# Attention tiles of the first batch pair loaded in 2 KB runs and turned by 64x64 products, in a chunked attention and low-rank mixer kernel

## The chip, the cores and the metric

The kernel runs on one core of a Trainium2 chip. The metric is the device time of one execution in microseconds (us), taken as the median of repeated runs; lower is better.

## What is computed

Eight batches (B) of eight heads (H), 576 tokens (S) and 64 channels per head (D). Attention works within chunks of 64 tokens; then a mixer works on the 512 channels (DM) of each token:

```python
# attention, per batch, head and chunk of 64 tokens
scores = q_c @ k_c.T / sqrt(64)
x = softmax(scores) @ v_c                    # heads side by side: x is [8, 576, 512]
# mixer
u = x + ((x.transpose(0, 2, 1) @ U) @ V).transpose(0, 2, 1)      # U is 576x32, V is 32x576
out = u + maximum(u @ w_ch1, 0) @ w_ch2      # w_ch1 is 512x2048, w_ch2 is 2048x512
```

q, k and v arrive as float32; U, V and the two weight matrices arrive as float64 words, and the kernel turns them into a high and a low part in fp32r.

## The kernel before

Two batches make a pair (`pr`), 1152 tokens, nine tiles of 128 tokens; three tiles make a group (`g`). Per pair and group there are 16 blocks (`f`, one for each 128 of the 2048 hidden channels): `hidden` (L823, 12 products of 384 columns), a relu split into a high part on ACT (L831, `hh`) and a low part on DVE (L836, `hl`), and `project_out` (L849, 9 products of 512 columns). There are 192 blocks in all, and TensorE does them one behind the other, the `out` of a block behind the `hidden` of the next.

**The planned part** is everything up to the 32nd block: groups 0 and 1 of the first pair in six stretches (`STRETCHES`), and all that must come before them. `LEAD` names the items in order of rank: `U` and `V` (the low-rank matrices), `W0` to `W15` (load and conversion of a weight slice: three steps on ACT, four on DVE), `T0` to `T8` (attention of the nine tiles of the first pair), `P0` and `P1` (x times U for either batch), `M0` and `M1` (mixes of groups 0 and 1), `S` (the split of U). `order()` is a list scheduler in Python with a cost for each operation and the rooms of the buffers; it gives one order per engine, and each engine works its own list strictly in order. DMAs are issued from SP (q, k, the second chunk of v, the weights), POOL (the first chunk of v, U, V) and ACT (`permute`).

**A planned tile** (`attention_ops`, L424 on): q and k arrive as [128 tokens, 8 heads, 64], so each run in DRAM is 256 B. Four products with the identity (L432, transpose mode, 128x128) turn each; ACT copies the result from PSUM (L442). Even heads end in the upper 64 partitions, odd heads in the lower. Then 16 scores products of 64x64 (L450, the two partition halves into two PSUM banks), maximum and subtraction on DVE, exp on ACT, four transposes of the weights, 16 products with v (L481; a column of ones in v, set by POOL at L410, gives the sums), and the scaling on DVE (L499). The buffers of q, k, v and of the turned q and k come from the tag `w`, which has 16 places and is shared with the weights.

**The agenda.** The tiles of the next pairs, and the third group (tiles 6 to 8) of the first, are worked in by hand at numbered slots, four to a block, so that slot 128 (`FIRST`) is the end of the planned part. `Tile` needs q and k in another order in DRAM, which `permute` (L655) writes: 16 DMAs of 288 KB for the second pair, each tied to the end of a `hidden` of the planned part (`gate`), here blocks 5 to 12 and every second of 14 to 28. `Tile.load` (L672) reads eight of them, and the first is at slot 68. `Mix` (L765 on) adds the low-rank term (L610, L616), turns 32x32 squares on DVE (L785), writes them to DRAM with four DMAs (`put`, L793), reads them back (`get`, L799), and splits them (L812 on ACT, L813 on DVE). The third group's mixes are at slots 97, 99 and 101 (`low_rank`, `add`), one slot later the turn, then `put`, and `get` at 102, 104 and 106; the splits are at 111 to 113.

Of the kernel before, what the change touches and what calls it, by code (L numbers as in the profile page):

```python
# [10 lines left out]
F32 = mybir.dt.float32  # L11
# [10 lines left out]
def kernel(  # L22
# [11 lines left out]
    nc = tc.nc  # L34
    B, H, S, D = q.shape
# [29 lines left out]
    work = ctx.enter_context(tc.tile_pool(name="work", bufs=1))  # L65
# [46 lines left out]
    def wslot(shape, dtype, name):  # L112
        return wpool.tile([P, *shape], dtype, tag="w", name=name, bufs=NF)
# [18 lines left out]
    def transfer(run, kb, *after, eng="SP", us=0.62, take="", free="", gbs=190.0):  # L132
        q = "dq" if eng == "SP" else "pq"
        o = Op(eng, us, run, *after, take=take + " " + q, lat=1.2 if eng == "SP" else 2.9)
        return Op("DMA", kb * 1.024 / gbs, lambda: None, o, free=free + " " + q, lat=0.5)

    ROOM = {"bank": 8, "w": NF, "slot": NS, "x": NX, "y": 2, "ut": 2, "h": 2, "mx": 2, "sm": 2, "dq": 8, "pq": 8}
    TICK = 3.4133

    def order():  # L140
        free_at = {}
# [9 lines left out]
        while ready:  # L151
# [238 lines left out]
    def early(pr, t):  # L390
        return pr == 0 and t < NEARLY

    loaded = {}
    begun = {}
    x_of = {}
# [1 line left out]
    ut_of = {}  # L397

    def load(pr, t, z):
        n = f"{pr}_{t}"  # L400
        if z == "q":
            if early(pr, t):
                words = wslot((4 * DM,), F32, "qkv_" + n)
                qn, kn = (words[:, z * DM : (z + 1) * DM].rearrange("p (h d) -> p h d", h=H) for z in range(2))
                vn = words[:, 2 * DM : 2 * DM + H * D1].rearrange("p (c a k) -> p c a k", c=2, k=D1)
            else:
                qn = slot(F32, "qn_" + n, (P, H, D))
                kn = slot(F32, "kn_" + n, (P, H, D))
                vn = slot(F32, "vn_" + n, (P, 2, HP, D1))
            nc.gpsimd.memset(vn[:, :, :, D:], 1.0)  # L410
            loaded[pr, t] = qn, kn, vn
        if z != "v":
            dst, src = (loaded[pr, t][0], q) if z == "q" else (loaded[pr, t][1], k_in)
            for r, m, b, s0 in segments(pr, t):
                nc.sync.dma_start(dst[r : r + m], src[b, :, s0 : s0 + m, :].rearrange("h s d -> s h d"))

    def load_v(pr, t, c, e):
        b, s0 = divmod(t * P + c * C, S)
        (nc.gpsimd if early(pr, t) and c == 0 else nc.sync).dma_start(
            loaded[pr, t][2][e * C : (e + 1) * C, c, :, 0:D],  # L420
            v[b + 2 * pr, e::2, s0 : s0 + C, :].rearrange("h s d -> s h d"),
        )

    def attention_ops(pr, t, after=None):  # L424
        n = f"{pr}_{t}"
        st = {}
        mine = early(pr, t)

        def transpose(src, name):
            ps = st[name] = bank("ps_" + name + n)  # L430
            for j in range(4):
                nc.tensor.transpose(ps[:, j * P : (j + 1) * P], src[:, j * P : (j + 1) * P], ident)  # L432

        def evacuate(name):
            if name[0] == "e" or not mine:
                dst = slot(F32, name + n, (P, HP, P))
            elif name[0] == "q":
                st["qk"] = wslot((2, HP, P), F32, "qkT_" + n)
                dst = st["qk"][:, 0]
            else:  # L440
                dst = st["qk"][:, 1]
            nc.scalar.copy(dst.rearrange("p a b -> p (a b)"), st[name])  # L442
            st[name] = dst

        def scores():
            ps = [bank(f"sc{e}_{n}") for e in range(2)]
# [48 lines left out]

        def scaled(e):
            if e == 0:
                st["x"] = work.tile([P, HP, 2, D], F32, tag="x", name="x_" + n, bufs=NX)
            nc.vector.tensor_mul(  # L499
                st["x"][:, :, e, :],  # L500
                st["av"][e][:, :, 0:D],
                st["sm"][:, e].unsqueeze(2).broadcast_to([P, HP, D]),
            )
            if e == 1:
                x_of[pr, t] = st["x"].rearrange("p a b k -> p (a b k)")

        src = lambda z: loaded[pr, t][z].rearrange("p h d -> p (h d)")
        flat = lambda: st["ex"].rearrange("p a b k -> p (a b k)")
        lq = transfer(lambda: load(pr, t, "q"), 256, after, take="w" if mine else "slot slot slot")
        lk = transfer(lambda: load(pr, t, "k"), 256, lq.after[0])  # L510
        lv, lq0 = lk, lq.after[0]
        vs = []
        for c in range(2):
            for e in range(2):
                lv = transfer(
                    lambda c=c, e=e: load_v(pr, t, c, e),
                    64,
                    (lk.after[0] if mine else lv.after[0]) if c else lq0,
                    eng="SP" if c or not mine else "POOL",
                )  # L520
                vs.append(lv)
        tq = Op("PE", 0.45, lambda: transpose(src(0), "qT_"), lq, begun.get((pr, t - 2)), take="bank")
        cq = Op("ACT", 0.48, lambda: evacuate("qT_"), tq, take="w" if mine else "slot", free="bank")
        tk = Op("PE", 0.45, lambda: transpose(src(1), "kT_"), lk, tq, take="bank")
        ck = Op("ACT", 0.48, lambda: evacuate("kT_"), tk, cq, take="" if mine else "slot", free="bank")
        sc = Op("PE", 0.58, scores, ck, take="bank bank", free="w" if mine else "slot slot slot slot")
# [5 lines left out]
        te = Op("PE", 0.45, lambda: transpose(flat(), "eT_"), ex, take="bank", free="slot")  # L532
        ce = Op("ACT", 0.48, lambda: evacuate("eT_"), te, take="slot", free="bank")
        av = Op("PE", 0.6, values, ce, *vs, take="bank bank x", free="slot w" if mine else "slot slot")
# [365 lines left out]

    LEAD = "U W0 T0 T1 T2 T3 T4 P0 T5 T6 V T7 T8 P1 M0 M1 W1 W2 W3 W4 W5 W6 S W7 W8 W9 W10 W11 W12 W13 W14 W15"
# [9 lines left out]
    for item in LEAD.split():  # L913
        rank[0] += 1
        z, i = item[0], int(item[1:] or 0)
# [51 lines left out]
    FIRST = 2 * NF * 4  # L967

    def at(s, *runs):
        agenda.setdefault(s, []).extend(runs)  # L970
# [8 lines left out]
        at(s + 6, a.get_ex)  # L979
        return a  # L980

    def plan_mix(pr, t, s):
        m = Mix(pr, t)
        at(s, m.low_rank, m.add)
        at(s + 1, m.turn)
        at(s + 2, m.put)
        at(s + 5, m.get)
        if pr:
            at(s + 10, m.split)
        return m  # L990

    def plan_proj(pr, e, i, s):
        if i == 0:
# [37 lines left out]
    for pr in range(1, NPAIR):  # L1031
# [5 lines left out]
        s = made[pr, 4] + 1  # L1037
# [4 lines left out]
        s = made[pr, 8] + 1  # L1042
# [68 lines left out]
```

## Time and profile before

| | us |
|---|---|
| median of 3 runs (938.71 to 943.48) | 943.03 |
| the profiled execution, its own time | 941.59 |
| its span, first to last instruction | 939.8 |

Of the span TensorE is busy 913.7 us (97%), VectorE (DVE) 457.9, ScalarE (ACT) 228.1, GpSimd (POOL) 82.2. The chain of work that ended last is TensorE for 91%; 84% of it are the two product lines of the blocks, L823 and L849. "Busy" counts a product from its start to its modelled end, so a busy TensorE need not be at its full rate, and what a stage costs beyond its products has to be read from the order of the products in that stage.

### The profile page before, as it was taken

What the parts mean: (1) busy time and instruction counts of PE and PEld (TensorE: products, weight loads), DVE (VectorE), ACT (ScalarE), POOL (GpSimd) and SP (SyncE); (2) the same over time, 40 slices, a digit from 0 to 9 for tenths busy, and PEclk for the clock granted to TensorE, in tenths of its full rate; (3) what the DMA queues carried; (4) which work ended last, traced back from release to release, by engine and by line L of the source; (5) the groups of instructions that cost most, each with busy time, mean ns of one, the idle gap of its engine ahead of it and who ended that gap; (6) DMA issues with size and microseconds to landing.
All of it is one profiled execution on the core that took longest, in us unless ns stands there. A gap on an engine that the chain in (4) does not pass through costs nothing.

```text
span 939.8 us, 16349 instructions
## 1 busy us (share of the span) xinstructions
PE 913.7 (97%) x6596; PEld 807.5 (86%) x6596; DVE 457.9 (49%) x901; ACT 228.1 (24%) x399; POOL 82.2 (9%) x147
## 2 busy tenths in 40 slices
PE   3999999989999999999999999999999999999998
PEld 2769888878888888888898888889899889999997
DVE  3788995555544555544534455543541533321211
ACT  4565771111221212211111122111221121111110
POOL 6000002021120101110010111120120100000000
PEclk9999999999999999999999999999999999999999
DMA  9984875464385574423455665531350312200000
GB/s 190 178 314 120 198 199 97 91 167 118 80 185 126 110 164 118 107 57 82 114 113 113 124 120 132 139 80 36 100 135 1 91 23 68 78 23 1 34 1 34
DMA packets 281211, 100.10 MB, mean 107 GB/s; under 512 B 206544, under 2 KB 268528, under 8 KB 281136
## 3 DMA queue, kind: packets, MB, share of 16 engines
q1 hardware_dynamic: 165440, 76.19, 32.2%
q10 hardware_dynamic: 111360, 14.16, 9.6%
q0 software_dynamic: 4336, 8.71, 3.7%
q8 instruction: 52, 0.85, 0.4%
q14 instruction: 23, 0.19, 0.1%
HBM read 74.63 MB, written 38.54 MB: 120 GB/s over the span
## 4 chain that ended last, share of the span: by engine, by line
PE 91%; DMA 4%; DVE 2%; SPq 1%; ACT 1%; issue 1%; ACTq 0%; DVEq 0%; POOL 0%
PE o L849 42%; PE h L823 42%; PE as L750 2%; DMA qkv<-in_k_dram 2%; PE as L697 1%; DMA wraw<-in_moe_w_ch_dram 1%; PE u L610 1%; PE y L564 1%; PE y L563 1%; DVE x L861 1%; PE y L569 1%; DMA kn<-kblocks 0%; DVE wraw L101 0%; DMA xs<-xb 0%; PE sc L450 0%
## 5 line engine op out<-in xcount | busy, mean ns | idle before, releaser
L823 PE MATMUL h<-uth,w 128*128 128x384 f32 x1536 | 424.0, 338 | 0.0
L849 PE MATMUL o<-w,hh 128*128 128x512 f32 x1152 | 364.1, 397 | 0.0
L836 DVE SCALAR_TENSOR_TENSOR hl<-h,hh 128x384 fp32r<-128x384 f32 x192 | 106.9, 557 | 382.3 <-ACT hh L831 382.2
L823 PEld LDWEIGHTS h<-uth,w 128*128 128x128 f32 x1536 | 281.2, 188 | 8.1 <-issue 0.2
L823 PE MATMUL h<-utl,w 128*128 128x384 f32 x768 | 259.6, 338 | 0.0
L849 PEld LDWEIGHTS o<-w,hh 128*128 128x128 f32 x1152 | 212.5, 188 | 35.3 <-ACT hh L831 0.4
L849 PE MATMUL o<-w,hl 128*128 128x512 f32 x576 | 227.9, 396 | 5.4 <-DVE hl L836 5.4
L831 ACT ACTIVATE hh<-h 128x384 fp32r<-128x384 f32 x192 | 94.3, 491 | 532.9 <-PE h L823 525.2
L823 PEld LDWEIGHTS h<-utl,w 128*128 128x128 f32 x768 | 144.2, 188 | 8.4 <-DVE utl L635 0.5
L849 PEld LDWEIGHTS o<-w,hl 128*128 128x128 f32 x576 | 108.4, 188 | 33.0 <-DVE hl L836 7.6
L687 POOL DMA_DIRECT2D vn<-in_v_dram x108 | 65.8, 616 | 649.6 <-DVE qT L680 131.3
L717 ACT ACTIVATE ex<-ex 128x512 f32<-128x512 f32 x27 | 17.1, 633 | 100.6 <-DVE ex L711 94.9
L710 DVE TENSOR_REDUCE mx<-as 128x4 f32<-128x256 f32 x54 | 22.7, 420 | 31.3 <-PE as L697 31.2
L861 DVE TENSOR_TENSOR x<-o,x 128x512 f32<-128x512 f32 x48 | 30.5, 679 | 5.1 <-PE o L849 5.1
L616 DVE TENSOR_TENSOR x<-u,x 128x512 f32<-128x512 f32 x36 | 23.9, 670 | 7.5 <-PE u L610 7.5
L813 DVE TENSOR_TENSOR utl<-uf,uth 128x512 fp32r<-128x512 f32 x30 | 20.4, 681 | 10.9 <-ACT uth L812 10.9
L711 DVE TENSOR_TENSOR ex<-as,mx 128x256 f32<-128x256 f32 x54 | 22.9, 425 | 1.9
L750 PEld LDWEIGHTS as<-vn,eT 64*64 64x64 f32 x864 | 15.4, 137 | 9.3 <-issue 9.3
L785 DVE STREAM_TRANSPOSE xb<-x 128x512 f32<-128x512 f32 x30 | 21.2, 706 | 0.6
L812 ACT CAST uth<-uf 128x512 fp32r<-128x512 f32 x30 | 18.2, 614 | 12.8 <-DMA uf<-xs 12.8
L556 DVE TENSOR_TENSOR xl<-x,xh 128x512 fp32r<-128x512 f32 x30 | 20.1, 681 | 1.0 <-ACT xh L552 0.7
L680 DVE STREAM_TRANSPOSE qT<-qn 128x512 f32<-128x512 f32 x27 | 18.9, 700 | 3.2 <-DMA qn<-qblocks 3.2
(87 smaller groups left out, 518.3 us busy)
## 6 DMA issues: line engine op xcount, KB each, us to landing
wraw<-in_moe_w_ch_dram SPq DMA_DIRECT2D x32, 512.0 KB, 5.3
out_dram<-x SPq DMA_DIRECT2D x36, 256.0 KB, 2.2
xs<-xb SPq DMA_DIRECT2D x120, 64.0 KB, 2.0
uf<-xs SPq DMA_DIRECT2D x30, 256.0 KB, 2.7
qblocks<-in_q_dram ACTq DMA_DIRECT2D x24, 288.0 KB, 4.3
kblocks<-in_k_dram ACTq DMA_DIRECT2D x24, 288.0 KB, 4.3
vn<-in_v_dram POOLq DMA_DIRECT2D x108, 64.0 KB, 2.8
exs<-exb SPq DMA_DIRECT2D x108, 64.0 KB, 1.8
```

The source lines that it names most:

```text
L616: nc.vector.tensor_add(x, st["u"], x)
L687: nc.gpsimd.dma_start(self.vn[e * C : (e + 1) * C, c], v[b + 2 * self.pr, HP * e : HP * (e + 1), s0 : s0 + C, :].rearrange("h s d -> s h d"),)
L710: nc.vector.reduce_max(mx[:, e], self.sc[e].rearrange("p (h k) -> p h k", k=C), axis=AX.X)
L711: nc.vector.tensor_sub(self.ex[:, e].rearrange("p b h k -> p h b k"), self.sc[e].rearrange("p (h b k) -> p h b k", b=2, k=TB), mx[:, e].un ...
L750: nc.tensor.matmul(ps[e][cs, (HP + hp) * C : (HP + hp + 1) * C], lhsT=self.eT[rows, hp, 2 * c : 2 * c + 2, :].rearrange("p a i -> p (a i)" ...
L785: nc.vector.transpose(self.xb.rearrange("p g (c t) -> p c g t", t=TB), x_of[self.pr, self.t].rearrange("p (c g k) -> p c g k", g=NQ, k=TB),)
L813: nc.vector.tensor_sub(ul, self.uf, uh)
L823: nc.tensor.matmul(ps[:, :GN], lhsT=w[:, z, cc], rhs=u[:, cc, :], start=(n == 0), stop=(n == 3 * NCC - 1))
L831: nc.scalar.activation(hh, ps[:, :GN], AF.Relu)
L836: nc.vector.scalar_tensor_tensor(hl, ps[:, :GN], 0.0, hh, op0=ALU.max, op1=ALU.subtract)
L849: nc.tensor.matmul(acc[j], lhsT=h[:, js], rhs=w2[f][:, z], start=(first and i == 0), stop=(final and i == 2),)
L861: nc.vector.tensor_add(x, ps, x)
```

## The change

1. q and k of a planned tile are loaded with partition = (head, run of 8 tokens), so that each partition is one contiguous run of 8 x 64 floats, 2 KB. For eight heads and 16 runs the DRAM side of the DMA has dimensions 8, 16 and 512. Tile 4, which spans two batches, takes two loads of 64 partitions for each.
2. They are turned by 16 products of 64x64 with the identity for each of q and k (no transpose mode), the upper 64 partitions to the upper half of the output and the lower to the lower, both halves into the same PSUM bank; the copy on ACT reads this bank with a permutation. Heads 0 to 3 are now in the upper half and 4 to 7 in the lower; v is loaded and x is laid out to match.
3. The planner's costs: 340 GB/s for these loads instead of 190, 0.55 us for a turn instead of 0.45.
4. The order `LEAD` is another one: T0 to T2 come first, W0 moves behind T5, S behind W8.
5. The 16 `permute` DMAs are tied to blocks 9 to 18 and to every second of 20 to 30.
6. The third group's mixes are at slots 83, 85 and 87 instead of 97, 99 and 101, with `get` at 103 to 105; the splits stay.
7. `early` is gone: it was true for all nine planned tiles.

```diff
-    NEARLY = 9
+    RUN = 8
+    LONG = 340.0
...
     def load(pr, t, z):
-            nc.sync.dma_start(dst[r : r + m], src[b, :, s0 : s0 + m, :].rearrange("h s d -> s h d"))
+            nc.sync.dma_start(
+                dst[r : r + m], src[b, :, s0 : s0 + m, :].rearrange("h (i j) d -> h i (j d)", j=RUN)
+            )
...
     def load_v(pr, t, c, e):
-            v[b + 2 * pr, e::2, s0 : s0 + C, :].rearrange("h s d -> s h d"),
+            v[b + 2 * pr, HP * e : HP * (e + 1), s0 : s0 + C, :].rearrange("h s d -> s h d"),
...
-            for j in range(4):
-                nc.tensor.transpose(ps[:, j * P : (j + 1) * P], src[:, j * P : (j + 1) * P], ident)
+            for j in range(RUN):
+                cs = slice(j * D, (j + 1) * D)
+                for e in range(2):
+                    if whole:
+                        rows = slice(e * C, (e + 1) * C)
+                        nc.tensor.matmul(ps[rows, cs], lhsT=src[rows, cs], rhs=ident[rows, rows], start=True, stop=True)
+                        continue
+                    nc.tensor.matmul(
+                        ps[e * C : (e + 1) * C, cs].rearrange("p (a c i) -> p c a i", a=HP, c=2),
+                        lhsT=src[:, cs],
+                        rhs=ident.rearrange("p (c b i) -> p c b i", c=2, b=2)[:, :, e],
+                        start=True,
+                        stop=True,
+                    )
...
+    def ordered(name):
+            nc.scalar.copy(
+                dst.rearrange("p a (i j) -> p a i j", j=RUN),
+                st[name].rearrange("p (j a i) -> p a i j", j=RUN, a=HP),
+            )
...
-    LEAD = "U W0 T0 T1 T2 T3 T4 P0 T5 T6 V T7 T8 P1 M0 M1 W1 W2 W3 W4 W5 W6 S W7 W8 ..."
+    LEAD = "T0 T1 T2 V T3 U T4 T5 W0 T6 T7 P0 T8 P1 M0 M1 W1 W2 W3 W4 W5 W6 W7 W8 S ..."
...
-            if 4 < blocks < 13 or blocks in range(14, 30, 2):
+            if 8 < blocks < 19 or blocks in range(20, 32, 2):
...
     for t in range(6, 9):
-        m = plan_mix(0, t, FIRST - 31 + 2 * (t - 6))
-        at(FIRST - 17 + t - 6, m.split)
+        plan_mix(0, t, FIRST - 45 + 2 * (t - 6), FIRST - 25 + t - 6)
```

## Rows read from the trace of the kernel before

**Rows 1.** The page: the span in 40 slices of 23.5 us, busy tenths of TensorE and of DVE.

```profile
PE   3999999989999999999999999999999999999998
...
DVE  3788995555544555544534455543541533321211
```

**Rows 2.** The windows view, all engines: window in us, its length, then busy us (and instructions) of PE, PEld, DVE, ACT and POOL, the granted TensorE clock (1.00 is full speed), DMA share, GB/s.

```profile
15.00:20.00 5.00, 2.18 (x9) 1.79 (x10) 2.70 (x3) 1.33 (x3) 2.81 (x7) 1.00 1.23 173
20.00:25.00 5.00, 4.06 (x46) 3.20 (x45) 3.50 (x8) 4.37 (x10) 1.34 (x3) 1.00 1.31 177
...
50.00:60.00 10.00, 9.57 (x150) 6.38 (x140) 8.36 (x26) 6.78 (x11) 0.00 (x0) 1.00 1.03 364
...
80.00:100.00 20.00, 18.53 (x94) 16.37 (x93) 16.97 (x22) 11.93 (x14) 0.00 (x0) 1.00 0.70 165
...
180.00:200.00 20.00, 17.57 (x128) 15.29 (x130) 8.16 (x14) 3.62 (x7) 2.44 (x4) 0.95 0.72 192
200.00:250.00 50.00, 49.77 (x444) 44.11 (x437) 29.47 (x68) 10.37 (x19) 7.31 (x12) 0.98 0.43 103
```

**Rows 3.** Waits, 0 to 30 us: who waited for whom, us in total, times, longest.

```profile
PE ps_qT L432 <- DMA qkv<-in_q_dram: 11.9, 2, 8.2
```

**Rows 4.** The instructions of the tile that holds q, k and v, to 60 us: the last line of that answer, the time from a DMA's issue to its landing.

```profile
DMA to landing us min/median/max: 2.6/6.2/11.5
```

**Rows 5.** Timeline of the lead-in (start, us, engine, line, operation; a bracket gives the idle time before it): the first load of q and its turn, the last tile's load of k and its turn, two of the copies on ACT, and products of the mix.

```profile
1.77 0.43 SPq L415 DMA_DIRECT2D qkv<-in_q_dram  x1
...
8.22 1.09 PE L432 MATMUL ps_qT<-ident,qkv 128*128 128x128 f32 x4 [8.22 <-DMA qkv<-in_q_dram]
...
35.04 0.58 ACT L442 COPY qkT<-ps_qT 128x512 f32<-128x512 f32 x1
...
42.63 0.58 SPq L415 DMA_DIRECT2D qkv<-in_k_dram  x1
...
50.18 0.66 PE L432 MATMUL ps_kT<-ident,qkv 128*128 128x128 f32 x4
...
53.81 0.94 PE L610 MATMUL u<-ys,vst 128*128 128x512 f32 x3
...
56.07 1.47 PE L622 MATMUL ut<-ident,x 128*128 128x128 f32 x12
```

**Rows 6.** The chain of waits followed back from 110 us (start, us, what): what one group of products takes when products stand right before and behind it, and where the blocks become continuous.

```profile
29.70 0.63 PE av L481 x32
...
31.39 0.62 PE sc L450 x32
32.01 0.69 PE vall L304 x4
...
34.43 0.44 PE ps_kT L432 x4
...
44.02 0.59 PE ps_eT L432 x4
...
45.04 0.86 PE y L569 x2
...
68.56 0.69 PE o L849 x3
69.25 4.22 PE h L823 x24
```

**Rows 7.** Timeline of ACT, 80 to 110 us: the issue of `permute` DMAs, and the conversion step behind them.

```profile
86.88 3.89 ACTq L655 DMA_DIRECT2D qblocks<-in_q_dram  x1
90.88 1.12 ACT L91 ACTIVATE wroom<-wraw 128x1024 f32<-128x1024 f32 x1 [3.95 <-issue]
```

**Rows 8.** Waits of TensorE alone, 80 to 100 us and then 180 to 200 us.

```profile
PE o L849 <- DVE hl L836: 1.5, 1, 1.5
PE o L849 <- DVE hl L836: 2.4, 1, 2.4
```

**Rows 9.** The chain of waits followed back from 260 us, the stretch around slots 100 to 113.

```profile
186.44 3.69 DMA xs<-xb
...
190.60 0.52 SPq L672
...
191.17 4.29 DMA kn<-kblocks
...
196.84 0.48 DVE hl L836
...
197.37 1.40 PE o L849 x4
```

**Rows 10.** Timelines of SP and of DVE, 154 to 180 us: the get of the first `Tile`'s weights (slot 83), the load of the second `Tile` (slot 86) and its turn on DVE (slot 91), then an `add` and a turn of the third group's mixes and the first `put`.

```profile
156.04 2.21 SPq L742 DMA_DIRECT2D eT<-exs  x4
158.30 0.53 SPq L672 DMA_DIRECT2D qn<-qblocks  x1
...
178.22 1.76 SPq L793 DMA_DIRECT2D xs<-xb  x4
166.10 0.70 DVE L680 STREAM_TRANSPOSE qT<-qn 128x512 f32<-128x512 f32 x1
...
178.11 0.65 DVE L616 TENSOR_TENSOR x<-u,x 128x512 f32<-128x512 f32 x1
178.80 0.71 DVE L785 STREAM_TRANSPOSE xb<-x 128x512 f32<-128x512 f32 x1
```

More of the change, by code (lines that the diff above doesn't have):

```diff
@@ L399, in load @@
     def load(pr, t, z):
-        n = f"{pr}_{t}"
         if z == "q":
[L402 to L409, printed above, removed]
-            nc.gpsimd.memset(vn[:, :, :, D:], 1.0)
-            loaded[pr, t] = qn, kn, vn
@@ L412, in load @@
-        if z != "v":
-            dst, src = (loaded[pr, t][0], q) if z == "q" else (loaded[pr, t][1], k_in)
-            for r, m, b, s0 in segments(pr, t):
-                nc.sync.dma_start(dst[r : r + m], src[b, :, s0 : s0 + m, :].rearrange("h s d -> s h d"))
+            words = wslot((4 * DM,), F32, f"qkv_{pr}_{t}")
+            vn = words[:, 2 * DM : 2 * DM + H * D1].rearrange("p (c a k) -> p c a k", c=2, k=D1)
+            nc.gpsimd.memset(vn[:, :, :, D:], 1.0)
+            loaded[pr, t] = words[:, 0:DM], words[:, DM : 2 * DM], vn
@@ L417, in load_v @@
+        dst, src = (loaded[pr, t][0], q) if z == "q" else (loaded[pr, t][1], k_in)
+        for r, m, b, s0 in segments(pr, t):
+            nc.sync.dma_start(
+                dst[r : r + m], src[b, :, s0 : s0 + m, :].rearrange("h (i j) d -> h i (j d)", j=RUN)
+            )
     def load_v(pr, t, c, e):
         b, s0 = divmod(t * P + c * C, S)
-        (nc.gpsimd if early(pr, t) and c == 0 else nc.sync).dma_start(
+        (nc.gpsimd if c == 0 else nc.sync).dma_start(
             loaded[pr, t][2][e * C : (e + 1) * C, c, :, 0:D],
-            v[b + 2 * pr, e::2, s0 : s0 + C, :].rearrange("h s d -> s h d"),
+            v[b + 2 * pr, HP * e : HP * (e + 1), s0 : s0 + C, :].rearrange("h s d -> s h d"),
@@ L422, in load_v, with attention_ops, by_heads, turned @@
         )
-    def attention_ops(pr, t, after=None):
+    def attention_ops(pr, t):
         n = f"{pr}_{t}"
         st = {}
-        mine = early(pr, t)
-        def transpose(src, name):
+        def by_heads(src, name):
             ps = st[name] = bank("ps_" + name + n)
+            whole = len(list(segments(pr, t))) == 1
+            for j in range(RUN):
[13 more added lines that the diff above has]
+        def ordered(name):
+            if name[0] == "q":
+                st["qk"] = wslot((2, HP, P), F32, "qkT_" + n)
+            dst = st["qk"][:, "qk".index(name[0])]
+            nc.scalar.copy(
+                dst.rearrange("p a (i j) -> p a i j", j=RUN),
+                st[name].rearrange("p (j a i) -> p a i j", j=RUN, a=HP),
+            )
+            st[name] = dst
+        def turned():
+            ps = st["eT_"] = bank("ps_eT_" + n)
+            src = st["ex"].rearrange("p a b k -> p (a b k)")
@@ L431, in transpose, with evacuate @@
             for j in range(4):
                 nc.tensor.transpose(ps[:, j * P : (j + 1) * P], src[:, j * P : (j + 1) * P], ident)
[L434 to L443, printed above, removed]
+        def evacuate():
+            dst = slot(F32, "eT_" + n, (P, HP, P))
+            nc.scalar.copy(dst.rearrange("p a b -> p (a b)"), st["eT_"])
+            st["eT_"] = dst
@@ L497, in scaled @@
             if e == 0:
-                st["x"] = work.tile([P, HP, 2, D], F32, tag="x", name="x_" + n, bufs=NX)
+                st["x"] = work.tile([P, 2, HP, D], F32, tag="x", name="x_" + n, bufs=NX)
             nc.vector.tensor_mul(
-                st["x"][:, :, e, :],
+                st["x"][:, e],
                 st["av"][e][:, :, 0:D],
@@ L504, in scaled @@
             if e == 1:
[L505 to L511, printed above, removed]
+                x_of[pr, t] = st["x"].rearrange("p b a k -> p (b a k)")
+        lq = transfer(lambda: load(pr, t, "q"), 256, take="w", gbs=LONG)
+        lk = transfer(lambda: load(pr, t, "k"), 256, lq.after[0], gbs=LONG)
         vs = []
@@ L517, in attention_ops @@
                     64,
-                    (lk.after[0] if mine else lv.after[0]) if c else lq0,
-                    eng="SP" if c or not mine else "POOL",
+                    lk.after[0] if c else lq.after[0],
+                    eng="SP" if c else "POOL",
                 )
                 vs.append(lv)
[L522 to L526, printed above, removed]
+        tq = Op("PE", 0.55, lambda: by_heads(loaded[pr, t][0], "qT_"), lq, begun.get((pr, t - 2)), take="bank")
+        cq = Op("ACT", 0.48, lambda: ordered("qT_"), tq, take="w", free="bank")
+        tk = Op("PE", 0.55, lambda: by_heads(loaded[pr, t][1], "kT_"), lk, tq, take="bank")
+        ck = Op("ACT", 0.48, lambda: ordered("kT_"), tk, cq, free="bank")
+        sc = Op("PE", 0.58, scores, ck, take="bank bank", free="w")
         m0 = Op("DVE", 0.42, lambda: maximum(0), sc, take="slot mx")
@@ L531, in attention_ops @@
         ex = Op("ACT", 0.53, exp, s1)
-        te = Op("PE", 0.45, lambda: transpose(flat(), "eT_"), ex, take="bank", free="slot")
-        ce = Op("ACT", 0.48, lambda: evacuate("eT_"), te, take="slot", free="bank")
-        av = Op("PE", 0.6, values, ce, *vs, take="bank bank x", free="slot w" if mine else "slot slot")
+        te = Op("PE", 0.45, turned, ex, take="bank", free="slot")
+        ce = Op("ACT", 0.48, evacuate, te, take="slot", free="bank")
+        av = Op("PE", 0.6, values, ce, *vs, take="bank bank x", free="slot w")
         sm = Op("DVE", 0.52, sums, av, take="sm")
@@ L980, in plan_tile, with plan_mix @@
         return a
-    def plan_mix(pr, t, s):
+    def plan_mix(pr, t, s, get=None):
         m = Mix(pr, t)
@@ L986, in plan_mix @@
         at(s + 2, m.put)
[L987 to L990, printed above, removed]
+        at(s + 5 if get is None else get, m.get)
+        at(s + 10 if get is None else get + 8, m.split)
     def plan_proj(pr, e, i, s):
```

4 lines of the change are left out of this document (1 added, 3 removed).

## The prediction

> **What bounds the kernel now.** I read the page's slices first [rows 1]: TensorE is at 9 tenths or more nearly everywhere, so only where it is not can much be won. That is the first slice, and within it the windows [rows 2] show TensorE busy for 2.2 us of 15 to 20 and 4.1 us of 20 to 25, while the DMA engines are at their full share and move only 173 to 177 GB/s. The waits [rows 3] name the cause: TensorE waits 11.9 us in two waits for q. So the lead-in is bound by loads of short runs; the first q is issued at 1.77 and turned at 8.22, the last k is issued at 42.63 and turned at 50.18 [rows 5]. From 50 us, with q and k in and weights alone under way (runs of 2 and 4 KB), the same engines move 364 GB/s [rows 2]. From 69.25 us on the blocks run one behind the other [rows 6], and everything later is TensorE's own time, but for two gaps: 1.5 us between 80 and 100 us, and 2.4 us between 180 and 200 us, both waits for `hl` from DVE [rows 8]. The second also costs clock: the granted clock is 0.95 over 20 us and 0.98 over the next 50 us [rows 2], some 2.0 us of full speed.
>
> **The lead-in today as a sum.** By 69.25 us one `hidden` and one round of `out`, 4.2 us, are done (half of what two blocks take: 24 products of `hidden` are 4.22 us [rows 6]), so the lead-in itself fills 65.0 us. TensorE's work in it, with the price of each group where it stands between others [rows 6]: 18 turns at 0.44 is 7.9; nine turns of the softmax at 0.59 is 5.3; nine scores at 0.62 and nine values at 0.63 is 11.3; ten products of `P` at 0.86 is 8.6; the spread of V is 0.7. From the timeline [rows 5], seven low-rank products at 0.31 are 2.2 and 24 transposes at 0.12 are 2.9. Together 38.9 us. Of 65.0 us, 8.2 go by before the first product, and 65.0 - 8.2 - 38.9 = 17.9 are waits and half rate: the first turn takes 1.09 us for what takes 0.66 later [rows 5].
>
> **The change part by part.**
> Loads. The bytes stay. A tile's q and k are 0.52 MB; at 175 GB/s that is 3.0 us, at the 364 GB/s of the weights 1.4 us. No row shows these loads in the new shape, so the ends are 175 and 364; I take 364, the row with the same run of 2 KB. With v (0.26 MB, still in 256 B runs, 1.5 us) a tile needs 2.9 us instead of 4.5. Nine tiles are 26 us, U, V and W0 (1.5 MB) some 4.5; from 2 us on the last tile is in at about 33. Today the same count gives 47, and the last turn is at 50.2; with those 3 us it is 36. Today's way from the last k's turn to the end of the lead-in is 65.0 - 50.2 = 14.8 us, which would end at 51: earlier than TensorE can be ready (below), so the loads no longer bind.
> First product. q goes first on SP, ahead of W0 and U. The quickest landing now is 2.6 us [rows 4]; issued at 1.2 us, the first turn is at 4.0 instead of 8.2.
> Turns. 16 products of 64x64, in 32 records like the scores. If they overlap as scores do, 0.62 us against 0.44: 18 x 0.18 = 3.2 us more of TensorE. Scores use all four quarters of the array and these only two. One record alone, from the transposes, takes 0.11 us for 128 columns, so 0.055 for 64, and 32 of them 1.76 us; two at once would be 0.88. Ends: 0.62 and 1.76 (3.2 and 23.8 us in all); I take 0.62, the row of the same shape.
> ACT's copy. 0.58 us today [rows 5]; a permuted read of PSUM isn't in the trace. From nothing to twice that, 18 x 0.58 = 10.4 us on an engine busy 11.9 of 20 us even in the later stage [rows 2]; I take nothing, since the copy has TensorE's other tiles beside it. v and x change only which head lies where: the same DMAs and operations, nothing.
> Order. W0, U and V move behind tiles on SP, POOL, ACT and DVE. Their conversions then lie beside attention instead of ahead of it; DVE is busy for 3 tenths of the first slice and 7 of the second [rows 1] and is not short. What of TensorE's waits stays: about 5 us of half rate at the start, as now (half of the 3 tenths of 23.5 us that it is busy in the first slice [rows 1], and some more behind it), and 6 us in which the first tiles' own chains, step by step over three engines, don't fill it. Ends for the two together: 5 and 15; I take 11.
> So the lead-in is 4.0 + 38.9 + 3.2 + 11 = 57.1, a gain of **7.9 us** (14 at best).
> The stage behind it is filled by DVE, which is busy 17.0 of 20 us [rows 2] with weights. It has to start earlier by as much; W1 is loaded by 40 us and its four steps on DVE find room, so I cost that at nothing; if not, the blocks wait for W1, and up to 4 us, one block, come back.
> `permute` later. At 86.88 the issue of one holds ACT for 3.89 us, and the conversion behind it starts 3.95 us late [rows 7]; DVE and `hl` follow, and TensorE stands 1.5 us. Moved by four blocks or more, they meet weights of which more are ready. Gain between 0 and 1.5; I take **1.5**. The first half is read from slot 68, block 18; its last DMA now follows block 16, two blocks, some 8 us, earlier, and a DMA of about that size lands in 4.29 [rows 9], so the load isn't held.
> Third group earlier. Today's chain at 186 us: the put of the last mix lands (3.69 us), only then SP issues the get, and behind it the next `Tile`'s load at 190.60, which takes 4.29 us; DVE, in order, stands before that turn, and behind it are the split and `hl`, on which `out` at 197.37 waits [rows 9]. With the puts 14 slots earlier the gets wait for nothing, and the load goes out some 4 us earlier. Worth 2.4 of idle time and 2.0 of clock; I take **3.9**, keeping half a microsecond for a turn that still comes close. Below nothing it can't be, since the same operations run.
> Where they go. Slots 83 to 89 get three `add` (0.65) and three turns (0.71) on DVE, 4.1 us, and twelve DMAs on SP, which takes 1.76 us for four. SP has there the get at 156.04 (2.21 us) and right behind it, at 158.30, the load of the second `Tile`, whose turn is due at 166.10 [rows 10]. The first put now stands between the two, and behind it the load may come 2 to 3 us later; 7.8 us of room become 5, against a landing of 4.3 [rows 9]. Cost between 0 and 4.4 (the stall of 186 us once more); I take **1.5**.
>
> **Sum.** 7.9 + 1.5 + 3.9 - 1.5 = 11.8 off the profiled execution's 941.6: 929.8. The median of the runs shown is 1.4 above that execution, so I forecast 931.2.
>
> **The rivals.**
> *Half the engines.* The new loads have only eight rows on the outermost dimension of the DRAM side; today's loads of q, k, v and the weights have 64 or more there. Should such a load be spread over half the DMA engines, 182 GB/s is left of 364: 0.52 MB takes 2.9 us, and a tile 4.4, as today. Then the change doesn't do what it says; the lead-in keeps what comes of the first q and the order, 2.5 us (0 to 5). The sum is 6.4, the time 936.6. For it: nothing in the trace limits the engines by shape, but no row has this shape. The Trainium skill (DMA: Bandwidth & Descriptors, "Why a DMA increments its semaphore by 16 and not by 1") states just this rule: the number of engines is the largest up to 16 that divides the slowest dimension of both sides. By it these loads get eight. No row here shows it.
> *Two at once.* The turns take 0.88: 4.7 us more than I took, of a lead-in that TensorE then binds; 935.9.
> *One at a time.* The two halves of a turn don't overlap, because both write one PSUM bank, while the scores' halves write two. 1.76 us a turn adds 20.6 us to my sum; some 4 of the waits fill up, and the time is 948. It cancels the gain from 1.3 us a turn on, and makes it slower by over 0.5% from about 1.55. Against it: the scores' 32 records take 0.62, so there they overlap. The Trainium skill (TensorEngine Tiling (Array Packing), "Restrictions and Gotchas") says that different row tiles cannot access the same PSUM bank simultaneously. No row here has two halves in one bank.
> *The stall moves.* The load behind the first put comes so late that DVE stands at slot 91 as it did at slot 113; the 3.9 are lost, and the time is 935.
>
> **How the numbers follow.** Chances: forecast 0.43, half the engines 0.27, two at once 0.11, the stall moves 0.08, one at a time 0.07, something else 0.04. The range takes in the best lead-in (14 + 1.5 + 4.4 less 0: 923) and the rivals up to 936.6 with some 4 us of W1 coming late: 923 to 941. A difference under 0.5% (4.7 us) can't be told from none here. Faster by more is all of the forecast, and about two thirds of the rivals near 936: 0.73; the same 0.20; slower 0.07.
>
> **What would show it.** A turn's 32 records in the timeline: 0.62, 0.88 or 1.76 us. GB/s in 5 to 30 us: near 300, or still under 200. The first product at 4 us, continuous blocks from about 61 us instead of 69.25. No wait for `hl` between 180 and 200 us and a clock of 1.00 there; none at slots 84 to 95 either. ACT's copy at 0.58. I am wrong if q still makes TensorE wait for ten microseconds, or if the weights' conversions hold the blocks once the lead-in is short.

## The result, and the profile after

The changed kernel takes 945.79 us (median of 7 runs, 944.92 to 947.72), the kernel before 940.82 beside it (7 runs): ratio 1.0056, interval 1.0037 to 1.0075. It is slower by half a per cent where 931.2 was forecast. Its profiled execution takes 945.79 us, with a span of 944.0, 4.2 us longer than before.

The page after: the span, and the slices that answer to [rows 1].

```profile
span 944.0 us, 17352 instructions
...
PE   5889999999999999999999999999999999999998
...
DVE  2679996455554455544533455543551533321211
```

The dip of before at slice 9 is gone. At the front the first slice rose from 3 to 5, but the two behind it stand at 8 where they stood at 9. The windows view after, columns as in [rows 2]:

```profile
10.00:15.00 5.00, 3.11 (x64) 2.73 (x64) 1.04 (x3) 0.58 (x1) 2.97 (x7) 1.00 0.73 175
15.00:20.00 5.00, 4.99 (x80) 4.70 (x84) 0.78 (x3) 2.35 (x6) 3.55 (x8) 1.00 0.72 186
20.00:25.00 5.00, 3.90 (x132) 3.51 (x131) 3.29 (x11) 2.50 (x6) 1.82 (x5) 1.00 0.65 172
25.00:30.00 5.00, 4.03 (x135) 3.51 (x134) 2.96 (x9) 2.33 (x6) 1.33 (x3) 1.00 0.68 173
50.00:60.00 10.00, 7.74 (x135) 4.88 (x133) 6.12 (x12) 5.43 (x9) 0.00 (x0) 1.00 1.00 349
...
180.00:200.00 20.00, 20.00 (x104) 18.38 (x104) 8.84 (x20) 4.22 (x8) 0.00 (x0) 1.00 0.66 161
200.00:250.00 50.00, 49.77 (x477) 43.52 (x477) 28.03 (x62) 10.20 (x19) 9.77 (x16) 1.00 0.45 106
```

From 10 to 30 us the rate is hardly more than it was, 172 to 186 GB/s against 173 to 177, but the DMA engines' busy share (next to last column) is 0.65 to 0.73 where it was 1.23 to 1.31 [rows 2]: with the longer runs the engines are not full. From 180 us on TensorE is full and its clock 1.00, against 17.57 of 20 us and 0.95. TensorE's groups by line and tile, 0 to 75 us, busy us and mean ns, then the idle time before them (the turns only; L430 is the tile that lies in two batches):

```profile
L428 PE MATMUL ps_qT<-ident,qkv 64*64 64x64 f32 x256 | 10.8, 244 | 7.6 <-POOL qkv L401 5.3 <-DMA qkv<-in_q_dram 2.1
L428 PE MATMUL ps_kT<-ident,qkv 64*64 64x64 f32 x256 | 10.7, 243 | 4.7 <-DMA qkv<-in_k_dram 4.7
...
L430 PE MATMUL ps_qT<-ident,qkv 128*64 128x64 f32 x32 | 1.2, 225 | 0.0
L430 PE MATMUL ps_kT<-ident,qkv 128*64 128x64 f32 x32 | 1.1, 223 | 0.0
```

18 turns take 10.8 + 10.7 + 1.2 + 1.1 = 23.8 us; the same view of before has 14.0 (7.1 for k, 6.9 for q). The 5.3 us that the view puts down to POOL are the wait for the first q: the first tile's step on POOL was done at 1.0 us, and in e2 below, with the same loads, the same view puts 5.5 us down to the load. With it TensorE waits 5.3 + 2.1 + 4.7 = 12.1 us for q and k. The timeline after answers to [rows 5]: the first turn, two later ones, an ACT copy, the last tile's turns.

```profile
5.34 1.97 PE L428 MATMUL ps_qT<-ident,qkv 64*64 64x64 f32 x32 [5.34 <-POOL qkv L401]
...
15.01 1.97 PE L428 MATMUL ps_qT<-ident,qkv 64*64 64x64 f32 x32 [1.13 <-DMA qkv<-in_q_dram]
...
20.71 1.15 PE L428 MATMUL ps_qT<-ident,qkv 64*64 64x64 f32 x32
...
43.36 0.56 ACT L442 COPY qkT<-ps_qT 128x512 f32<-128x512 f32 x1
...
56.22 1.15 PE L428 MATMUL ps_qT<-ident,qkv 64*64 64x64 f32 x32
57.21 1.03 PE L428 MATMUL ps_kT<-ident,qkv 64*64 64x64 f32 x29
```

The last k is turned at 57.21 instead of 50.18. The chain of waits of the first 60 us hangs on q and k now (three long pieces and a turn; start, us, what):

```profile
4.32 12.38 DMA qkv<-in_k_dram
...
16.71 11.31 DMA qkv<-in_k_dram
...
32.62 9.09 DMA qkv<-in_q_dram
...
44.68 0.93 PE ps_kT L428 x32
```

So from 20 us on a turn is 0.93 to 1.15 us.

Where the time went is plainest block by block: the start of each block's first `hidden` in the timeline of the one profiled execution, less the same of before (us; before at 60.45, 81.71, 98.36, 151.71, 160.68, 190.10 and 201.85):

| kernel | block 1 | 5 | 9 | 21 | 23 | 30 | 31 to the end |
|---|---|---|---|---|---|---|---|
| after | +10.8 | +10.3 | +8.4 | +8.4 | +9.1 | +8.3 | +4.35 |
| e4_before_later | -0.3 | -0.3 | -2.2 | -1.9 | -1.3 | -2.1 | -6.0 |
| e8_leadonly (e4 and the new order) | -4.6 | +3.35 | +1.4 | +1.4 | +2.1 | +1.3 | -2.6 |

The lead-in loses 10.3 us by block 5; the permutes give back 1.9 (block 9), the crowd of the earlier mixes takes 0.7 (block 23) and gives most of it back by block 30, the third group gives 4.0 (block 31).

### The profile page after: what moved, and what is told of

It reads as the page before. It is cut to its first block, busy times and chain, and to the rows that moved or that the text cites. A ratio compares the mean times of both kernels' runs of the same rounds, so it can differ in the third digit from the quotient of the medians.

```text
span 944.0 us, 17352 instructions
## 1 busy us (share of the span) xinstructions
PE 920.5 (98%) x7100; PEld 816.6 (87%) x7100; DVE 458.1 (49%) x901; ACT 228.5 (24%) x399; POOL 82.6 (9%) x147
## 4 chain that ended last, share of the span: by engine, by line
PE 90%; DMA 4%; DVE 3%; ACT 1%; SPq 1%; issue 1%; DVEq 0%; ACTq 0%
PE o L860 42%; PE h L834 42%; DMA qkv<-in_k_dram 3%; PE as L761 2%; PE as L708 1%; DMA wraw<-in_moe_w_ch_dram 1%; DMA qkv<-in_q_dram 1%; PE u L621 1%; PE y L575 1%; PE y L574 1%; DVE x L872 1%; DVE wraw L101 0%; SPq L405 0%; SPq L411 0%; DVE utl L646 0%
## 5 line engine op out<-in xcount | busy, mean ns | idle before, releaser
L375 DVE TENSOR_TENSOR w<-wroom,w 128x1024 fp32r<-128x1024 f32 (+1 forms) x19 | 19.7, 1051 | 2.0 <-ACT w L372 1.9
L823 ACT CAST uth<-uf 128x512 fp32r<-128x512 f32 x30 | 18.2, 614 | 8.5 <-DMA uf<-xs 8.3
```

## The experiments

Theory A was that the loads use half the DMA engines and hold TensorE, theory B that the turns bind, theory C that the new order does. Two measures stand side by side below. The ratio to before rests on all executions of a run. "Block 5" is the start of the fifth block against before, in us, in the one profiled execution, and executions of one kernel differ: those of e1 take 941.68 to 950.38 us, the longer ones on the whole at a lower mean clock (0.998 down to 0.994).

**e5_alone**, loads and turns by themselves: eight loads of q (2.1 MB) in each of three shapes, one shape after the other, and eight turns of each of six kinds. It computes nothing of the reference.

> The disputed costs by themselves; nothing of the reference is computed, the output is filled with zeros. SP loads eight pieces of q of 256 KB (128 partitions of 2 KB) with the DRAM side as 8, 16, 512, then as 16, 8, 512, then in runs of 256 B, then the first two again, each lot of 2.1 MB with nothing beside it. Then TensorE turns eight pieces in each of six ways. If 8 outer rows reach half the engines: some 12 us a lot at 0.5 of the engines for the first, 6 us at full share for the second, 10 to 12 for the short runs. If the shape doesn't matter: 6 us for both. Turns: 0.9 to 1.0 us as the change does them (the halves overlap two at a time); with the two halves one behind the other in the list 1.8 if nothing but overlap of halves helps; with two banks the same as now if the bank is not the limit, 0.6 or less if it is; in four quarters 0.5 to 0.6; four transposes 0.44.

Windows while the loads of one shape are under way (no engine computes; the last three columns are clock, DMA share, GB/s): the change's shape, the runs of 8 tokens outermost (16 rows), the old 256 B runs, the change's again.

```profile
3.00:13.00 10.00, 0.00 (x0) 0.00 (x0) 0.00 (x0) 0.00 (x0) 1.00 0.51 191
21.00:28.00 7.00, 0.00 (x0) 0.00 (x0) 0.00 (x0) 0.00 (x0) 1.00 1.05 258
36.00:46.00 10.00, 0.00 (x0) 0.00 (x0) 0.00 (x0) 0.00 (x0) 1.00 1.20 206
53.00:63.00 10.00, 0.00 (x0) 0.00 (x0) 0.00 (x0) 0.00 (x0) 1.00 0.52 196
```

And its timeline, eight turns of each kind in a row: as in the change; first one half of the rows, then the other; halves in two PSUM banks; the halves of rows and of columns on all four quarters (this row: four turns); all rows with half the columns; four transposes of 128x128.

```profile
116.66 7.68 PE L59 MATMUL now<-ident,x_rows 64*64 64x64 f32 x256
124.17 12.23 PE L59 MATMUL inrow<-ident,x_rows 64*64 64x64 f32 x253
...
136.41 7.46 PE L59 MATMUL twobanks<-ident,x_rows 64*64 64x64 f32 x250
...
146.14 2.09 PE L89 MATMUL quarters<-ident,x_rows 64*64 64x64 f32 x128 [0.34 <-issue]
...
149.85 7.68 PE L99 MATMUL allrows<-ident,x_rows 128*64 128x64 f32 x256
157.47 3.71 PE L107 MATMUL four<-ident,x_rows 128*128 128x128 f32 x32
```

The change's load has a busy share of 0.51, the same bytes with 16 rows outermost 1.05; the price is 191 to 196 GB/s against 258, and the old short runs had 206. I had expected 6 us for the 2.1 MB with 16 rows, some 350 GB/s; that fell. That 8 outer rows reach eight engines is the rule of the Trainium skill (DMA: Bandwidth & Descriptors, "Why a DMA increments its semaphore by 16 and not by 1"): the trace agrees, 0.51 against 1.05. A turn is 7.68 / 8 = 0.96 us against 0.46. Only two of the products run at a time, and the bank is not the reason: 7.68 in one bank, 7.46 in two (the row leaves out six of its 256 records), but 12.23 one half after the other (1.53 a turn, where I had expected 1.8) and, on all four quarters, 2.09 for four turns, 0.52 each. Where the Trainium skill (TensorEngine Tiling (Array Packing), "Restrictions and Gotchas") says that row tiles cannot access one bank simultaneously, these two rows show no slowdown from it.

**e1_rows16** undoes the half engines alone, **e2_turns4** the slow turn alone, **e3_both** both:

```diff
 e1, e3: load
-src[b, :, s0 : s0 + m, :].rearrange("h (i j) d -> h i (j d)", j=RUN)
+src[b, :, s0 : s0 + m, :].rearrange("h (i j) d -> i h (j d)", j=RUN)
 e2, e3: by_heads, in place of the 16 products
+for j in range(4):
+    nc.tensor.transpose(ps[:, j * P : (j + 1) * P], src[:, j * P : (j + 1) * P], ident)
```

> The changed kernel with one thing different: the DRAM side of the q and k loads lists the 16 runs outermost and the 8 heads behind them (16, 8, 512 instead of 8, 16, 512). Same bytes, same runs of 2 KB, same plan, same products; rows come to other partitions, so the attention of the first pair is computed from mixed-up rows. If the loads are slow because 8 outer rows reach only half the DMA engines: GB/s between 10 and 30 us rises from about 175 to 250 or more, q and k no longer hold TensorE, and 8 to 14 us go (932 to 938). If 2 KB runs in loads of this size are slow whatever the order of dimensions, or if the turns hold TensorE: within 3 us of the changed kernel (943 to 949).

> The changed kernel with each turn of q and k done by four 128x128 transposes as before, with the plan's costs and order untouched; the loads stay in the new shape, so the attention of the first pair is computed from wrongly turned data. If TensorE is what holds the lead-in: 18 turns at about 1.0 us become 0.44 to 0.66, so 7 to 10 us go (936 to 939). If the loads or the order of the lists hold it: at most 3 us go (943 to 946).

> Both edits of the two kernels beside it: 16 outer rows and four transposes for a turn (first pair computed from wrong data). If the loads and the turns are all that went wrong, this shows what I forecast with 0.62 for a turn, or 3 us better: 927 to 932. If the order of the lists, planned for other times, costs something of its own, it stays above 934 although both causes are gone.

| | ratio, interval | block 5 | profiled execution less median, us | half clock, us |
|---|---|---|---|---|
| after | 1.0056 (1.0037 to 1.0075) | +10.3 | 0.0 | 0 |
| e1_rows16 | 1.0052 (1.0024 to 1.008) | +6.2 | -2.6 | 1.7 |
| e2_turns4 | 1.001 (0.9994 to 1.0027) | +8.45 | +1.2 | 3.4 |
| e3_both | 0.9949 (0.9933 to 0.9965) | +3.7 | +2.5 | 5.1 |

"Half clock" is what the granted clock under 1.00 comes to in the windows of 10 us up to 80 us: a window at 0.83 is 1.7 us of full speed. Before has none there.

By the ratios 16 outer rows alone give back 0.4 us, quick turns alone 4.3, both 10.1, nearly all of the 11.4 between after and e4 (0.9935, below): A and B together are the loss, and the pair is worth more than its parts. By block 5 the three are 4.1, 1.85 and 6.6, hardly more than the parts; but e1's profiled execution was its fastest and e3's its slowest, so the single shares are not settled.

In e1 the rate did not rise to 250 GB/s as I expected, though the share did:

```profile
15.00:20.00 5.00, 5.00 (x164) 4.70 (x160) 3.00 (x9) 4.11 (x10) 2.55 (x7) 1.00 1.12 207
20.00:25.00 5.00, 3.59 (x98) 3.08 (x99) 3.12 (x10) 2.02 (x4) 3.33 (x8) 1.00 0.86 180
```

(The tile that lies in two batches keeps 8 outer rows in either order: its pieces of 64 tokens are 8 runs.) The waits for q and k fall from 12.1 to 7.2 us, and the turns stay at 11.1 + 10.8 + 1.4 + 1.2 = 24.5 us. In e2, TensorE's waits to 60 us (who waits for whom, us, times, longest):

```profile
PE ps_qT L423 <- DMA qkv<-in_q_dram: 9.3, 5, 5.5
PE ps_kT L423 <- DMA qkv<-in_k_dram: 9.1, 6, 3.3
```

Its turns are busy 13.5 us instead of 23.8, but the waits for q and k grow from 12.1 to 18.4, and the granted clock is 0.83 from 30 to 40 and from 50 to 60 us: most of what the turns save goes there. What stays in e3 lies, as far as its trace shows, in the clock. Its waits for q and k to 75 us come to 14.4 us, as in before (11.9 + 2.9), but from 20 to 50 us the granted clock is 0.83 where before has 1.00. Why it falls here and not there isn't shown. The waits and three windows of e3:

```profile
PE ps_kT L423 <- DMA qkv<-in_k_dram: 7.8, 5, 2.6
PE ps_qT L423 <- DMA qkv<-in_q_dram: 6.6, 2, 4.7
```

```profile
20.00:30.00 10.00, 6.13 (x117) 5.00 (x116) 5.44 (x16) 3.81 (x7) 3.61 (x8) 0.83 0.96 180
30.00:40.00 10.00, 7.86 (x153) 6.34 (x154) 5.93 (x20) 5.29 (x9) 0.00 (x0) 0.83 1.05 230
40.00:50.00 10.00, 10.00 (x157) 6.93 (x156) 7.31 (x17) 7.61 (x14) 0.00 (x0) 0.83 0.94 272
```

**e7_oldlead** (after with the old `LEAD`), **e8_leadonly** (before with the new `LEAD` and the two late edits) and **e6_replan** (after with the planner's prices set to what was measured) test C.

```diff
 e6
-LONG = 340.0
+LONG = 175.0
-tq = Op("PE", 0.55, ...)      (tk the same)
+tq = Op("PE", 1.0, ...)
```

> The changed kernel with the items ranked as before (U and W0 first, V behind T6). If the new order of items is what hurts: 3 us or more less than the changed kernel, 943 or below. If it helps, as I took it to by bringing the first q 4 us forward: 3 to 5 us more, 949 to 951.

> The kernel before with the later permutes, the earlier mixes and the new order of items; loads in 256 B runs and turns by four transposes as before. Against the run with the first two of these alone (934.9). If the new order brings the first q forward and so helps: 2 to 4 us less, 931 to 933. If it hurts, because W0 and W1 then come late for the first blocks: 937 or more.

> The changed kernel with the planner told other costs: 175 GB/s for the loads of q and k instead of 340, 1.0 us for a turn instead of 0.55. The work is the same; only the order in the lists differs. If a good part of the loss comes from lists that were made for loads and turns twice as quick (ACT and DVE standing before steps whose data are not in): 4 to 8 us less than the changed kernel, 938 to 942. If the loads and the turns alone set the lead-in: within 2 us of it.

e7 1.0075 (1.0052 to 1.0099), block 5 at +10.5: with the change's loads and turns the old order is no better than the new one, which the change has at 1.0056 and +10.3. e8 0.9968 (0.9949 to 0.9988), block 5 at +3.35 beside e4's -0.3: the new order costs 3.6 us with the old loads and turns (3.1 by the ratios). e6 1.0042 (1.0017 to 1.0066), block 5 at +8.7: the prices alone return 1.6, which the intervals don't tell from nothing. In e8, TensorE's waits from 52 to 92 us, three windows of 2 us around them, and ACT's timeline ahead of the first:

```profile
PE h L823 <- DVE utl L635: 1.8, 1, 1.8
PE o L849 <- ACT hh L831: 1.7, 1, 1.7
```

```profile
60.00:62.00 2.00, 0.65 (x2) 0.30 (x2) 2.00 (x5) 2.00 (x3) 0.00 (x0) 1.00 1.01 331
...
64.00:66.00 2.00, 2.00 (x5) 1.07 (x4) 2.00 (x2) 0.59 (x1) 0.00 (x0) 0.50 0.04 16
...
78.00:80.00 2.00, 2.00 (x8) 2.00 (x7) 2.00 (x3) 1.90 (x3) 0.00 (x0) 0.50 0.00 0
```

```profile
57.77 1.19 ACT L94 ACTIVATE wraw<-wraw 128x1024 uint32<-128x1024 uint32 x1
59.86 1.05 ACT L371 CAST w<-wroom 128x1024 fp32r<-128x1024 f32 x1 [0.90 <-issue]
60.81 0.48 ACT L831 ACTIVATE hh<-h 128x384 fp32r<-128x384 f32 x1
```

Its first block starts 4.6 us sooner, but `hh` stands on ACT behind steps of the next weights' conversions, and DVE is full in the same windows (third busy column) and late with `utl`. After each wait the granted clock falls to 0.50, the lower of its two levels; from 60 to 80 us it is 0.83 on the mean, 3.4 us of full speed. The head start is spent, and 3.35 more.

**e4_before_later**, **e9_permutes**, **e10_mixes**: the kernel before with the late edits, both and each alone.

```diff
 e4, e9
-if 4 < blocks < 13 or blocks in range(14, 30, 2):
+if 8 < blocks < 19 or blocks in range(20, 32, 2):
 e4, e10
-m = plan_mix(0, t, FIRST - 31 + 2 * (t - 6))
-at(FIRST - 17 + t - 6, m.split)
+plan_mix(0, t, FIRST - 45 + 2 * (t - 6), FIRST - 25 + t - 6)
```

> The kernel before with only two parts of the change: the 16 permute DMAs tied to the later blocks and the third group's mixes 14 slots sooner. Loads, turns and lead-in as before. If the stalls at 90 and 190 us are what those parts remove: 4 us for the mixes and 1.5 to 2 for the permutes, 934 to 936, with no wait for hl between 180 and 200 us. If those stalls go only because the longer lead-in shifts the DMAs against each other: 939 to 942.

> Before with the later permutes alone. If the two gains add up, the 1.9 us of the stall at 88 to 96 us come back and nothing else: ratio 0.998, the wait for hl between 180 and 200 us still there. If one of the two was only worth something with the other (the permutes moved now meet the third group's turns on DVE), 1.000 and no gain left behind block 31.

> Before with the third group's mixes earlier alone. If the gains add up, 4.0 us come back at block 31 (2.4 of idle time and the half rate behind it): ratio 0.9957, the wait for hl at 90 us still there. If the later permutes carry the gain of both edits together, no more than 0.999.

e4 takes 934.85 us, 0.9935 (0.9914 to 0.9957): the parts of the change that touch neither loads nor lead-in, and faster than both kernels. e9 0.9969 (0.9955 to 0.9984), e10 0.9958 (0.9942 to 0.9974). By blocks: e9 gains 1.9 at block 9 and another 1.4 at block 31, though the mixes are where they were; e10 loses 0.7 at block 23 and gains 4.1 at block 31. The 1.4 are not a shorter wait. TensorE still stands 2.5 us for `hl` from 180 to 200 us, where before has 2.4; what differs is the clock, 1.00 in this execution of e9 where before has 0.95 [rows 2]:

```profile
180.00:200.00 20.00, 17.49 (x145) 15.21 (x144) 9.61 (x18) 4.07 (x8) 2.44 (x4) 1.00 0.82 210
```

As far as the waits go, the two gains add up. (Block 5, untouched in all three, lies 0.3 to 1.0 us ahead of before: so much of the lead-in differs between these executions.)

**e11_both_oldlead**, **e12_both_oldlead_220**, **e13_both_220**: e3 with the old order, e11 with the one price 340 changed to 220 GB/s, e3 with that price. What is left in e3 is asked here.

```diff
 e12, e13
-LONG = 340.0
+LONG = 220.0
```

> After with quick turns and loads over all the engines (the kernel e3_both) and the old order of the lead-in. The attention of the first pair is from mixed-up rows. If the new order costs by itself (W0's conversion put between attention's and weights' steps on DVE, which then makes TensorE wait twice near 60 and 74 us), the old order ends the lead-in as before or earlier: blocks from the fifth on no later than before, ratio 0.9935, as before with the two late edits alone; if the loads' 250 GB/s against 218 are worth something too, 0.991. If the order costs only together with the old loads, no better than e3_both: 0.995 or more, the fifth block some 3.7 us late.

> The kernel e11_both_oldlead (quick turns, loads over all the engines, old order of the lead-in; attention of the first pair from mixed-up rows) with the planner's price of the loads of q and k at 220 GB/s instead of 340. If the price is what makes ACT stand at a weight that has not landed, that wait goes (3.8 us) and with it TensorE's 3.6 us for the softmax; the fifth block comes no later than before, ratio 0.993 to 0.994. If the loads themselves bind, the fifth block stays some 4 us late and the ratio at 0.998.

> The kernel e3_both (the same, with the new order of the lead-in) with the price at 220 GB/s. If the price is the cause: ACT's wait of 2.0 us for a weight goes, the fifth block comes 2 to 4 us sooner, ratio 0.991 to 0.993. If the new order or the loads bind: 0.995 as e3_both.

| | order, price | ratio, interval | block 5 | profiled execution less median, us | half clock, us |
|---|---|---|---|---|---|
| e11_both_oldlead | old, 340 | 0.9984 (0.9972 to 0.9996) | +4.05 | +0.1 | 3.4 |
| e12_both_oldlead_220 | old, 220 | 0.9913 (0.9882 to 0.9944) | -3.4 | -0.6 | 0 |
| e3_both | new, 340 | 0.9949 (0.9933 to 0.9965) | +3.7 | +2.5 | 5.1 |
| e13_both_220 | new, 220 | 0.998 (0.9962 to 0.9999) | +5.6 | +1.8 | 3.4 |

My expectation for e11, that the old order cures e3, fell. Its waits from 25 to 60 us:

```profile
ACT wroom L91 <- DMA wraw<-in_moe_w_ch_dram: 3.8, 1, 3.8
PE ps_eT L439 <- ACT ex L473: 3.6, 1, 3.6
```

ACT, in order, stands at the conversion of a weight that has not landed, and the softmax that TensorE needs is queued behind it. Before has no such wait of ACT in the lead-in. With the price at 220 it is gone in e12, and the lead-in ends 3.4 us earlier than before: the one kernel here in which long runs shorten it, though with turns that leave wrong rows. e13 was expected to gain as well and lost 1.9 (2.9 by the ratios): the same price that mends the old order hurts the new one. In its trace TensorE is busy for 5.35 us from 20 to 30 and 6.68 us from 30 to 40 us, and then has 0.74 of the full clock:

```profile
40.00:50.00 10.00, 10.00 (x155) 6.84 (x154) 6.13 (x15) 5.77 (x10) 0.00 (x0) 0.74 0.98 298
```

**e14_rows16_right** is e12 with turns that compute the right thing from those loads (16 products, all rows, 0.95 us in the planner); **e15_replan_old** is e6 with the old order.

```diff
 e14: by_heads
+half = ident.rearrange("p (i e a) -> p e i a", e=2, a=HP)
+    lhsT=src[:, cs], rhs=half[:, e]      (8 j, 2 e)
```

> After with loads over all the engines in the order (8 tokens, head) and turns that sort the heads while turning (16 products of 128x64, so the right result), prices of 220 GB/s and 0.95 us in the planner, and the old order of the lead-in. If price and order were the loss, this is e12_both_oldlead_220 with turns of 0.94 instead of 0.46 us: e1 against e3 put those at 2.6 us, so the fifth block some 1 us earlier than before and a ratio of 0.993 to 0.995. If turns of 0.94 bind the lead-in (18 x 0.48 = 8.6 us), the fifth block is 5 us late and the ratio 1.000.

> After with the planner's prices at what was measured (175 GB/s, 1.0 us a turn) and the old order of the lead-in; loads on half the engines and turns as in the change. If the order made for wrong prices is most of the loss: 6 us better than e6_replan, ratio 0.998 and the fifth block 2 to 3 us late. If loads and turns bind: within 2 us of e6_replan, ratio 1.002 to 1.006.

e14 1.0034 (1.0017 to 1.0052), block 5 at +7.7; e15 1.0083 (1.0056 to 1.011), block 5 at +14.8. Both came out worse than I expected. e14 from 30 to 40 us, and its turns from 0 to 75 us:

```profile
30.00:40.00 10.00, 10.00 (x239) 7.08 (x238) 5.50 (x19) 4.05 (x8) 0.00 (x0) 1.00 0.83 188
```

```profile
L426 PE MATMUL ps_qT<-ident,qkv 128*64 128x64 f32 x288 | 11.9, 244 | 11.2 <-DMA qkv<-in_q_dram 11.2
L426 PE MATMUL ps_kT<-ident,qkv 128*64 128x64 f32 x288 | 11.5, 237 | 0.3 <-issue 0.3
```

Its turns take 23.4 us where e12's take 13.7, and TensorE is full from 30 to 40 us. Against e12 it loses 11.0 us at block 5 (11.4 by the ratios). The two differ in the turn, and with it in the turn's price in the planner and so in the lists; that the turn itself binds fits, but no run separates it from the lists.

## Why the prediction was wrong, point by point

**The loads: wrong.** The first step that failed is the price of the new loads: of the ends 175 and 364 I took 364, the weights' row, and concluded that the loads no longer bind. Measured are 172 to 186 GB/s from 10 to 30 us, 191 to 196 alone, and TensorE still waits 12.1 us for q and k. The row was not even of the same run. Before, 50 to 60 us:

```profile
DMA packets 2427, 3.64 MB, mean 364 GB/s; under 512 B 112, under 2 KB 2017, under 8 KB 2426
```

By the kernel these are runs of 1 KB (128 words of 8 bytes) and 4 KB, not 2. Nor was it of the same outermost rows, on which my rival had it: alone, 8 or 16 of them make 191 or 258 GB/s. But that is only a part. Over all engines 2 KB runs of q stay at 258, and in the kernel (e1) at 180 to 207; what holds them there is not shown.

**The turns: wrong.** 0.62 was the row of the same shape, but of a step that uses four quarters of the array, which the text itself said. The middle rival (0.88) had the mechanism, two products at a time: 0.96 alone, 0.93 to 1.15 in the kernel, 23.8 us for 18 against a forecast of 11.1. On all four quarters a turn does take 0.52 (e5).

**The sum of the lead-in.** Forecast: 4.0 to the first product, 31.0 of other work (38.9 less today's turns, 7.9), 11.1 of turns, 11 of waits and half rate, 57.1. After: 65.0 + 10.3 = 75.3, that is 5.3 + 31.0 + 23.8 and 15.2 left for waits. Of the 18.2 us missed, 1.3 are the first product (q needs 4.6 us from its issue at 0.74, not 2.8), 12.7 the turns and their half rate, 4.2 waits. (The first four turns take some 3.3 us more than later ones; the forecast had such half rate in its 11, not in the turns.) That is an account of the critical engine, not a price list: in e2 quicker turns alone bring 1.85 at block 5, and 4.3 by the ratios.

**The rivals.** Half the engines had the mechanism, the share and the rate right, and gave 936.6, because it kept a gain of 2.5 us in the lead-in and priced the turns at 0.62. Two at once was right as well. They came together, which I had not worked out; by their own prices the lead-in would lose 4.7 - 2.5 = 2.2 us, of the 10.3 measured. One at a time did not happen: halves in one bank overlap.

**The order: taken as no cost, wrong in part.** With the old loads and turns it costs 3.6 us (e8 against e4), by the weights' conversions on ACT and DVE, which I named as what would prove me wrong and priced at nothing, and by the clock behind the two waits. In the change itself it costs nothing that shows (e7). It is not bad as such: with the change's loads, turns and true prices it is 6.0 us better than the old one (e6 against e15, block 5; 3.9 by the ratios), with quick loads and turns and the price 220 it is 9.0 us worse (e13 against e12; 6.3 by the ratios). Which order is better hangs on durations and prices together; no run shows a rule for it.

**ACT's copy: right.** 0.56 to 0.59 us.

**Permutes, third group, crowd: right.** Forecast 1.5, 3.9 and -1.5; measured 1.9, 4.0 and -0.7, the last mostly given back. The waits for `hl` shrink to one of 0.5 us at 80 to 100 and to none at 180 to 200 us, and the clock there is 1.00. They are the whole gain of the change, and without its loads, turns and order (e4) it is 6.0 us. This part I had from the waits in the trace, and e4, e9 and e10 bear it out.

**Open.** Why long runs of q over all engines stay at 258 GB/s alone and near 200 in the kernel, where the weights have 349 to 364; how the loss divides between loads and turns; and why a price nearer the measured one makes the new order worse (e13). Turns on all four quarters (0.52 us alone) were not tried in the kernel; in e5 they write two banks and leave the turned pieces in other places.

## What to carry to other kernels

Before you price a new transfer, look whether the profile has a row with its outermost rows as well as its run: a load can have long packets and use half the engines, and the DMA share beside GB/s tells it (0.7 at the old rate). When a change makes a load cheaper and a step on the engine dearer, price the two together, since mending one can turn into waits for the other (0.4 and 4.3 us alone, 10.1 together, by the ratios). Look at the granted clock in every stretch behind a wait before you look for a third cause. An order of items has to be measured again whenever durations or prices change, and late, independent edits are tested by themselves, as they may be all of the gain. When one execution is profiled, see where it lies among the others before you read shares from it.

## What the runs showed of the hardware

- A load with 8 outer rows kept a share of 0.51 of the DMA engines at 191 GB/s; with 16 outer rows, same packets, 1.05 and 258.
- 16 products of 64x64 on two quarters take 0.96 us in one PSUM bank and as long in two, 1.53 when one half's products all come before the other's, 0.52 on four quarters in two banks, and 0.96 as 128x64; four 128x128 transposes 0.46.
- In the kernel the same 16 outer rows brought 180 to 207 GB/s at a share of 0.86 to 1.13, against 172 to 186 at 0.65 to 0.73 with 8.
- In the first 20 us after the start a turn took 1.97 us and later 1.15, while the column of granted clock read 1.00 in both windows: there it does not show the slower rate.
- Behind waits of TensorE in the lead-in the granted clock fell to 0.50 (e8, 64 to 66 us) with TensorE full; in e3 it was 0.83 from 20 to 50 us, 5.1 us of full speed.
